# A 2-D spectral filter with a gate: products of both column halves in one tensor, stage 6 in two row tiles

## The chip, the cores and the metric

The kernel runs on one core of one Trainium2 chip. The metric is device time in microseconds of one execution. The core has a matrix engine (PE, with a weight-load stream of its own that the profile calls PEld), three elementwise engines (DVE, ACT, POOL), a queue that mostly issues transfers (SP), and 16 DMA engines. They run side by side and wait for each other through semaphores. Products of PE go to PSUM, eight banks of 512 float32 values on each of 128 partitions; everything else lies in SBUF.

## The reference

The input `x` is one matrix of 2048 rows and 1024 columns in bfloat16. Two filters A and B, each with a real and an imaginary weight of 2048 x 513, are applied to its 2-D spectrum, and a gate per row mixes the two results. The reference calls the same function twice, with A's weights and with B's, on the same `x`:

```
g = _sigmoid((x * gate_w).sum(-1, keepdims=True))
X = jnp.fft.rfft2(x.astype(jnp.float32), axes=(-2, -1))
X = X * (w_r + 1j * w_i)
y = jnp.fft.irfft2(X, s=(S, D), axes=(-2, -1)).astype(jnp.bfloat16)
return g * a + (1 - g) * b        # a: y with A's weights, b: y with B's
```

## The kernel before, in words

All transforms are matrix products with constant matrices, and the 2048 rows are split as 32 x 64 (row = 64 n1 + n2). The stages:

- Stages 1 and 2 load and fold `x` (`fold`), and transform it along n1 (`stage1`) and along the columns (`fold3`, `stage2`).
- Stage 4 (`stage4`) transforms along n2. It runs in 16 steps. Step i belongs to one half `hf` of the column frequencies and to one block `p` of two row frequencies; `SEQ` gives the order of the (hf, p) pairs. Each step leaves a spectrum tile X(i) in the buffer `XF`, copied out of PSUM by ACT (by DVE in steps 3 and 7). `swap` then copies X(i) to `MM` by DMA with neighbouring partitions exchanged, so that real and imaginary parts can be multiplied crosswise. POOL issues the swaps of steps 0 to 8, SP those of steps 9 to 15. There are six buffers (`NX`) for X and for its swapped copy.
- `product` multiplies X(i) (`sw` 0) or its swapped copy (`sw` 1) by the weights on DVE. The weights lie in `WA`, 64 rows (32 row frequencies for A, 32 for B) of 514 values, each row seen as two column halves of 257. With `sw` 0 the result goes to a second tensor `WB`, with `sw` 1 it goes over the weights in `WA`. One product covers both column halves of its columns. `ORDER` lists which products are put into DVE's queue after each step; entries are (step, sw, first half-block, half-blocks, steps). A half-block is 64 of the 128 columns of a `hf`.
- Weights come in six key groups (`wload`, keys 0 to 5: row frequencies in blocks 0, 1-3, 4-7, 8-11, 12-13, 14-15), 44 transfers issued by SP in that order. `product` waits for the key of its block. `save512` moves the column 512 of the weights out of the way and puts column 256 in its place; its second call (k = 1) reads the keys 1 to 5. It is called after step 9's products.
- Stage 5 (`group_mm`, `group_out`) transforms back along n2: 32 groups of 16 matmuls. Group g handles 8 columns; groups 1 to 15 and then 0 use `hf` 0, groups 16 to 31 use `hf` 1. Groups 1 to 7 need the lower half-blocks of all eight `hf` 0 products, groups 8 to 15 the upper ones, and likewise for `hf` 1. Step 14 stands ahead of group 1, step 15 behind the second group done. The result Z goes to `WB`, out of PSUM by ACT, a few by DVE.
- The gate: `row_sums` and `zsum` give the row sums of x times `gate_w`, ACT takes the sigmoid, and `gate_mask` writes it in two versions, one for each column half, with zeros at the other half's partitions. `rbgen` multiplies the constant `U5` by it, 1024 values for each of 16 r, half of them zero.
- Stage 6 (`stage6_mm`) transforms back along n1, mixing A and B: for each of 16 values of r, 16 matmuls with Z as weights and the scaled constant as moving operand. The contraction runs over 128 partitions (filter, row frequency, column half); the zeros keep the two column halves apart. Its output Y goes to `WA`.
- Stage 7 (`stage7`) transforms back along the columns. In the plain form PE works on half of the columns that the full form has, and ACT, DVE and POOL unfold them by sums and differences (POOL L837). The `half` form (r = 5, 9, 12) does one of the two unfoldings on PE, the `full` form (r = 14, 15) both; these leave POOL out. Outputs go to a ring of six buffers (`NOU`) and from there to memory by SP.

The order on each engine is the order of the `P.add` calls, written by hand, and every engine works strictly in that order. The class `Prog` derives the waits from keys: `r` reads, `w` writes, `a` adds to a key's writers. The lines that matter most here are these two loops (L676 to L687):

```
    for i in range(STEP5):
        step(i)
        ...
        products(i)
        if i in (1, 9):
            save512(i // 8, 0)
            save512(i // 8, 1)
```

Of the kernel before, what the change touches and what calls it, by code (L numbers as in the profile page):

```python
# [10 lines left out]
RW, HW = 514, 257  # L11
RWS = (528, RW)
# [13 lines left out]
def make_consts():  # L26
# [83 lines left out]
    l2, sl_, f = row % 2, (row // 2) % 32, row // 64  # L110
# [11 lines left out]
    SM[:, 1], SM[:, 2] = l2 == 0, l2 == 1  # L122
# [112 lines left out]
def bass_gated_mix__spectral_gfnet__spectral_gfnet__prompt_kernel(nc, A_x, A_w_r, A_w_i, B_x, B_w_r, B_w_i, gate_w, out):  # L235
# [7 lines left out]
    WA = sb("WA", 64 * RW)  # L243
    WB = sb("WB", 64 * RWS[0])
    FT = sb("FT", 16384)
    XF = sb("XF", 9216)
    MM = sb("MM", 6144)
    F2 = sb("F2", 2048)
    EO = sb("EO", 1024)
# [8 lines left out]
    VD = sb("VD", 1024)  # L258
# [4 lines left out]
    WT = (WB, WA)  # L263
# [32 lines left out]
    def xloc(c):  # L296
        return WT[c // 2], ((c % 2) * 32 + 24) * RWS[c // 2]

    XPARTS = {0: ((0, 1), (1, 1), (2, 2)), 1: ((0, 2), (2, 2)), 2: ((0, 2), (2, 2)), 3: ((0, 2), (2, 2))}
    XALL = [("x", c, q0) for c in range(4) for q0, n in XPARTS[c]]  # L300
# [25 lines left out]
    def wload(key, t0, t1):  # L326
        n = t1 - t0 + 1
        runs = ((t0, 2 * t0, n, 1), (32 - t0, 2 * t0 + 1, n, -1)) if t0 else ((0, 0, 2, 16),)
        for k0, s0, n, st in runs:
            for f in range(2):  # L330
                for ri in range(2):
                    src = wsrc[f, ri]
                    s = AP(src.tensor, src.offset + k0 * 513, [[32 * 513, 64], [st * 513, n], [1, 513]])
                    d = sl(WA, (f * 32 + s0) * RW, [(2 * RW if t0 else RW, n), (1, 513)], p0=ri, np_=64, pstep=2)
                    dma("sp", f"w{key}", d, s, a=[("W", key)] + XALL * (t1 >= 12))
        for t in range(t0, t1 + 1):
            need[t] = key
# [81 lines left out]
    NX = 6  # L419
# [6 lines left out]

    def fblock(cmb, j, t):
        if cmb in (1, 2):
            return sl(FT, cmb * 4096 + j * 2048 + t * 128, [(1, 128)])
        if t < 4:  # L430
            return sl((EO, VD)[t // 2], cmb // 3 * 512 + j * 256 + t % 2 * 128, [(1, 128)])
        return sl(FT, cmb * 4096 + j * 2048 + (t - 4) * 128, [(1, 128)])

    def ekeys(i, cs, s):
        return [("E", i, cs, s)] + ["VD"] * (i == 1)

    def fold3(i, css=(0, 1)):

        n = len(css)
        for s, op in enumerate((ALU.add, ALU.subtract)):  # L440
            src = [sl(FT, 12288 * css[0] + j * 2048 + i * 256, [(12288, n), (1, 256)]) for j in range(2)]
            dst = sl(FT, 12288 * css[0] + s * 2048 + (i - 2) * 256, [(12288, n), (1, 256)]) if i > 1 else sl((EO, VD)[i], 512 * css[0] + 256 * s, [(512, n), (1, 256)])
            P.add("dve", lambda e, dst=dst, src=src, op=op: e.tensor_tensor(out=dst, in0=src[0], in1=src[1], op=op),
                  r=[("F1a" if i < 2 else "F1", cs, j) for cs in css for j in range(2)] + [("FR", i, j) for j in range(2)],
                  w=[("E", i, cs, s) for cs in css] + [("FR", i - 2, s)] * (i > 1), a=["VD"] * (i == 1))
# [28 lines left out]
    def stage4(i):  # L474
# [12 lines left out]
        if i in (3, 7):  # L487
# [10 lines left out]
    def product(i, sw, h0=0, n=2, ni=1):  # L498

        hf, p = SEQ[i]  # L500
        steps = range(i, i + ni)
        assert all(SEQ[k] == (hf, p + k - i) and Xk(k) == Xk(i) + k - i for k in steps)
        xt, xo, xk = (MM, XSo(i), "XS") if sw else (XF, Xo(i), "X")
        at = lambda k: sl(WT[k], 4 * p * RWS[k] + 128 * hf + 64 * h0, [(32 * RWS[k], 2), (RWS[k] // 2, 8 * ni), (1, 64 * n)])
        P.add("dve", lambda e: e.tensor_tensor(out=at(sw), in0=sl(xt, xo + 64 * h0, [(0, 2), (128, 8 * ni), (1, 64 * n)]), in1=at(1), op=ALU.mult),  # L505
              r=[(xk, Xk(k)) for k in steps] + [("c256", p > 0)] * hf + [("W", need[t]) for t in range(2 * p, 2 * (p + ni))],
              a=[("prod", sw, hf, h) for h in range(h0, h0 + n)])
# [23 lines left out]
    def row_sums():  # L531
        vt = sl(VD, 0, [(1, 1024)]).bitcast(f32)
        P.add("dve", lambda e: e.tensor_tensor(out=vt, in0=sl(CL, VCo, [(1, 512)]), in1=sl(GSB, 0, [(0, 32), (2, 16)]), op=ALU.mult),
              r=["CV", "GSB"], w=["VD"])
        P.add("dve", lambda e: e.tensor_reduce(AT[:], vt.rearrange("p (n t) -> p n t", t=16), axis=mybir.AxisListType.X, op=ALU.add),
              r=["VD"], w=["AT"])
        P.add("dve", lambda e: e.tensor_copy(AB[:], AT[:]), r=["AT"], w=["AB"])

    def save512(k, part):

        s0, n = ((0, 4), (4, 28))[k]
        at = lambda l: sl(WA, s0 * RW + l, [(32 * RW, 2), (RW, n)])
# [12 lines left out]

    GMo = lambda r: (XF, 7168 + r * 256) if r < 8 else (MM, 4096 + (r - 8) * 256)

    def zsum(us):
        for k, u in enumerate(us):
            for n in range(16):  # L560
# [4 lines left out]
                  r=[bank(2 * u), bank(2 * u + 1), "SM"], **({"a" if k else "w": [("CS", 0), ("CS", 1)]}))  # L565

    def gate_mask(hf):
        t, o = GMo(8 * hf)
        for h in range(2):
            P.add("dve", lambda e, h=h: e.tensor_scalar(  # L570
                out=sl(t, o + h * 32, [(64, 32), (1, 32)]), in0=sl(XF, 1024 * hf, [(32, 32), (1, 32)]),
                scalar1=SM[:, 1 + h:2 + h], scalar2=None, op0=ALU.mult),
                r=[("CS", hf), "SM"], w=[("GM", hf, h), ("XS" if hf else "X", 4), ("XS" if hf else "X", 5)])


    def col0(u, sw):
        t = WT[sw]
# [4 lines left out]
        for q, (tt, to, st) in enumerate(((t, 0, RWS[sw]), (PST, sw * 64, 1))):  # L582
# [7 lines left out]
        P.add("act", lambda e: e.activation(sl(t, 0, [(RWS[sw], 64)]), ps(o0, [(1, 64)]), ACT.Copy),  # L590
# [3 lines left out]
    RBS = [(FT, (4 + k) * 2048 + 1024, []) for k in range(4)] + [(F2, 1024 * k, ["F2"]) for k in range(2)]  # L594
    RBS += [(XF, 1024 * k, [("CS", k)]) for k in range(3)] + [(XF, 3072 + 1024 * k, [("X", k)]) for k in range(4)]
    RBS += [(MM, 1024 * k, [("XS", k)]) for k in range(4)]

    def rbgen(r, eng, after=()):
        t, o, k = RBS[r]
        g, go = GMo(r)  # L600
        return P.add(eng, lambda e: e.tensor_tensor(
            out=sl(t, o, [(256, 4), (64, 4), (32, 2), (1, 32)]),
            in0=sl(FT, U5o + (r // 2) * 2048 + (r % 2) * 512, [(128, 4), (32, 4), (0, 2), (1, 32)]),
            in1=sl(g, go, [(0, 4), (64, 4), (32, 2), (1, 32)]), op=ALU.mult),
            r=["U5", ("GM", r // 8, 0), ("GM", r // 8, 1)], w=[("RB", r)] + k, after=[last2] + list(after))

    def group_mm(u, g, qs, at):
        hf = g // 16
        for q in qs:
            l0 = 8 * g + q  # L610
            o = ps(u * 1024 + at(q) * 128, [(1, 128)])
            for ab in range(2):
                deps = [("prod", ab, hf, g // 8 % 2), "CL"] + [("col0", ab)] * (g == 0)
                P.add("pe", lambda e, o=o, l0=l0, ab=ab: e.matmul(  # L614
                    o, sl(WT[ab], l0, [(RWS[ab] // 2, 128)]), sl(CL, KIo[ab], [(1, 128)]), start=(ab == 0), stop=(ab == 1)),
                    r=deps, w=[bank(2 * u + at(q) // 4)])

    def group_out(u, g, eng, q0, n, st, at, keys):
        src = ps(u * 1024 + at * 128, [(1, 128), (128, n)])
        dst = sl(WB, 8 * g + q0, [(RWS[0] // 2, 128), (st, n)])  # L620
# [36 lines left out]
    def step(i):  # L657
# [5 lines left out]
        if i == 15:  # L663
# [3 lines left out]
    ORDER = (((0, 0),), ((1, 0),), (), ((2, 0), (3, 0)), ((0, 1), (4, 0)), ((1, 1),), (), ((2, 1), (3, 1)),  # L667
             ((5, 0, 0, 2, 2), (4, 1), (5, 1, 0, 2, 2), (7, 0), (7, 1)), ((8, 0, 0, 1), (8, 1, 0, 1), (8, 0, 1, 1)), ((8, 1, 1, 1), (9, 0, 0, 2, 2)), ((9, 1, 0, 2, 2),), ((11, 0, 0, 2, 2),),
             ((11, 1, 0, 2, 2),))
# [38 lines left out]
    product(13, 0, 0, 2, 2)  # L708
    star_products()
# [3 lines left out]
    for a in ((13, 1, 0, 2, 2), (15, 0, 0, 1), (15, 1, 0, 1), (15, 0, 1, 1), (15, 1, 1, 1)):  # L713
        product(*a)
    row_sums()
# [8 lines left out]
    for n, g in enumerate(range(16, 32)):  # L724
        if n == 14:
            last_groups([spare(), spare()])
        elif n < 14:
            group(spare(), g, "dve" if n == 1 else "act")
        if n == 1:
            zsum([spare(), spare()])  # L730
            gate_mask(0)
            gate_mask(1)
            for _ in range(12):
# [6 lines left out]
    Yo, PQo = 0, 16384  # L740
    EOo = PQo + NPQ * 2048
    OUo = EOo + 2 * 1024
    assert OUo + NOU * 1024 <= 64 * RW

    def stage6_mm(r, bs, pis):
        b0 = 6 * (r % 2)
        t6, o6, _ = RBS[r]
        for b in bs:
            for pi in pis:
                for cp in range(2):  # L750
                    n = cp * 64 + 16 * b + r
                    lh = sl(WB, n * (RWS[0] // 2) + pi, [(2, 128)])
                    rh = sl(t6, o6 + cp * 512 + b * 64, [(256, 2), (1, 64)])
                    o = ps(b0 * 512 + b * 256 + pi * 128, [(1, 128)])
                    P.add("pe", lambda e, o=o, lh=lh, rh=rh, cp=cp: e.matmul(o, lh, rh, start=(cp == 0), stop=(cp == 1)),  # L755
                          r=[("Z", pi), ("RB", r)], w=[bank(b0 + b // 2)])

    def stage6(r, mm=True):
        b0 = 6 * (r % 2)
        if mm:  # L760
            stage6_mm(r, range(4), range(2))
        for k in range(2 if r == 0 else 1):
            n = 2 if r == 0 else 4
            src = ps((b0 + k) * 512, [(32, 8), (1, 32), (256, n)])
            dst = sl(WA, Yo + r * 128 + 2 * k, [(2048, 8), (4, 32), (1, n)])
            kw = dict(r=[bank(b0 + k + q) for q in range(n // 2)], a=[("Y", r)], after=[last5])
# [5 lines left out]
    HALF = (5, 9, 12)  # L772
    pqc = 0

    def stage7(r):
        nonlocal pqc
        full, half = r >= 14, r in HALF
        b0 = 6 * (r - 14) if r >= 14 else 4 - 2 * (r % 2)
        oo = OUo + (r % NOU) * 1024
        es = sl(WA, EOo + (r % 2) * 1024, [(1, 1024)]).bitcast(f32)  # L780

        def mm(col, c0, n, ri, pi, h, k, last):
            lh = sl(WA, Yo + (pi * 4 + ri * 2 + h) * 2048 + r * 128, [(1, 128)])
# [4 lines left out]
        def ods(s, k, n):  # L788
            return sl(WA, oo + 1023 * s + 512 * (1 - 2 * s) * k, [(512 * (1 - 2 * s), n), (1 - 2 * s, 256)])
# [11 lines left out]
        if full:  # L801
# [3 lines left out]
            for k0, n, bk in ((0, 2, b0),) if r == 14 else ((0, 1, b0), (1, 1, 4)):  # L805
                for k in range(4):
                    mm(bk * 512, k0, n, 0, k // 2, k % 2, k, 3)
                finals(k0, n, bk, WA, EOo + (r % 2) * 1024, [("EO", r % 2)])
        elif half:
# [7 lines left out]
            for s, op in enumerate((ALU.add, ALU.subtract)):  # L817
                P.add("dve", lambda e, s=s, op=op: e.tensor_tensor(out=sl(MM, to + s * 512, [(1, 512)]).bitcast(f32),
                                                                   in0=ps((b0 + 1) * 512, [(1, 256)]), in1=es[:, :256], op=op),
                      r=[("EO", r % 2), bank(b0 + 1)], w=[("T", r % 2, s), ("GM", 1, 0), ("GM", 1, 1)])  # L820
            finals(0, 2, b0, MM, to, [("T", r % 2, 0), ("T", r % 2, 1)])
        else:
# [7 lines left out]
            pq = PQo + pk * 2048  # L830
            for s, op in enumerate((ALU.add, ALU.subtract)):
                P.add("dve", lambda e, s=s, op=op: e.tensor_tensor(out=sl(WA, pq + s * 1024, [(1, 1024)]).bitcast(f32), in0=ps(b0 * 512, [(1, 512)]),  # L832
                                                                   in1=es, op=op),
                      r=[("EO", r % 2), bank(b0)], w=[("PQ", pk, s)], after=[last5])
            pv = sl(WA, pq, [(1, 2048)]).bitcast(f32).rearrange("p (a b c) -> p a b c", a=2, b=2)
# [6 lines left out]
        if r < 15:  # L842
            return [store("act" if r == 14 else "sp", f"o{r}", outv[:, r, :], sl(WA, oo, [(1, 1024)]), (0, 1))]
# [84 lines left out]
```

## Time and profile before

| | |
|---|---|
| median of 3 runs | 122.58 us (122.23 to 122.69) |
| profiled execution | 122.14 us, of which the span from first to last instruction is 120.1 us |
| PE / weight loads | 114.1 us busy (95%) / 95.9 us (80%) |
| DVE / ACT / POOL | 99.5 us (83%) / 99.0 us (82%) / 38.4 us (32%) |
| granted PE clock | 0.996 |
| DMA | 26.1 MB, mean 217 GB/s |

Busy times are shares of the whole span; the stages have different limits. Matmuls are pipelined, so a matmul's "busy" (219 ns for 128 columns) is its time in the pipeline, and the pace at which they follow each other is read from the chain or from start times. "L505" is line 505 of the kernel. In the groups an operation is shown with its output and inputs by the program's names. An idle time in brackets is the time that the engine sat before the instruction, and behind the arrow stands what ended it.

### The profile page before, as it was taken

To read this page: it belongs to the slowest core of one execution; us is meant where nothing else is said; L and a number is where in the kernel's file an instruction comes from. 1 tells how busy PE (TensorE), PEld (TensorE's weight loads), DVE (VectorE), ACT (ScalarE), POOL (GpSimd) and SP (SyncE) were. 2 spreads that over 40 slices of the span, in tenths; PEclk is the share of its full clock that TensorE was granted. 3 is DMA by queue.
4 is the path that set the end of the run, shared out by engine and by line. 5 is a ranking of instruction groups with operands and counts; after the bars stand their busy time and mean duration, and the time that the engine had idled before them with its cause. 6 is when DMAs were issued, how large, how long until landed. Compare 5 with 4: busy or idle time off the path is not lost.

```text
span 120.1 us, 3690 instructions
## 1 busy us (share of the span) xinstructions
PE 114.1 (95%) x1556; PEld 95.9 (80%) x1556; DVE 99.5 (83%) x160; ACT 99.0 (82%) x119; POOL 38.4 (32%) x47
## 2 busy tenths in 40 slices
PE   6998999999999999999999999999999999999960
PEld 4676889787675675689999999999899979898630
DVE  0568999988999999999999949995695687787890
ACT  4249998999797999899999989999779868867710
POOL 1000010036575500000000000000029999999980
PEclk9999999999999999999999999999999999999998
DMA  2999999999999999832699500000000422434456
GB/s 84 328 394 421 415 331 366 349 350 352 361 369 364 360 370 368 321 137 85 162 392 394 199 0 5 0 5 0 0 5 8 158 96 93 175 124 160 160 222 215
DMA packets 17680, 26.11 MB, mean 217 GB/s; under 512 B 2112, under 2 KB 11072, under 8 KB 17664
## 3 DMA queue, kind: packets, MB, share of 16 engines
q1 hardware_dynamic: 16368, 23.00, 54.6%
q0 software_dynamic: 864, 2.36, 5.4%
q10 hardware_dynamic: 432, 0.52, 1.4%
q8 instruction: 12, 0.20, 0.7%
q14 instruction: 4, 0.03, 0.1%
HBM read 17.48 MB, written 4.19 MB: 180 GB/s over the span
## 4 chain that ended last, share of the span: by engine, by line
PE 59%; SPq 18%; DMA 9%; DVE 8%; issue 3%; ACT 1%; POOL 0%; DVEq 0%; POOLq 0%
PE PS L614 26%; SPq L290 18%; PE PS L785 14%; PE PS L755 11%; DMA WA<-in_B_w_i_dram 9%; DVE WA L505 3%; PE PS L304 3%; DVE WB L505 3%; PE PS L387 2%; DVE WA L796 1%; PE PS L561 1%; PE PS L482 1%; PE PS L588 1%; ACT WB L625 1%; DVEq L867 0%
## 5 line engine op out<-in xcount | busy, mean ns | idle before, releaser
L837 POOL TENSOR_TENSOR WA<-WA 128x512 bf16<-128x512 f32 x22 | 27.6, 1290 | 48.2 <-DVE WA L832 48.2
L614 PE MATMUL PS<-CL,WB 128*128 128x128 bf16 x256 | 31.8, 226 | 0.0
L614 PE MATMUL PS<-CL,WA 128*128 128x128 bf16 x256 | 31.7, 223 | 0.1
L614 PEld LDWEIGHTS PS<-CL,WB 128*128 128x128 bf16 x256 | 31.3, 145 | 0.3 <-DVE WB L505 0.2
L614 PEld LDWEIGHTS PS<-CL,WA 128*128 128x128 bf16 x256 | 31.3, 145 | 0.3 <-DVE WA L505 0.2
L625 ACT ACTIVATE WB<-PS 128x1024 bf16<-128x1024 f32 (+1 forms) x31 | 28.8, 1042 | 0.2 <-PE PS L614 0.2
L770 ACT ACTIVATE WA<-PS 128x1024 bf16<-128x1024 f32 (+1 forms) x16 | 15.8, 996 | 6.2 <-PE PS L755 6.1
L505 DVE TENSOR_TENSOR WB<-XF,WA 128x2048 bf16<-128x2048 bf16 (+2 forms) x14 | 19.3, 1384 | 1.0 <-ACT XF L490 0.5
L785 PE MATMUL PS<-FT,WA 128*128 128x256 bf16 (+1 forms) x132 | 19.3, 292 | 0.1
L505 DVE TENSOR_TENSOR WA<-MM,WA 128x2048 bf16<-128x2048 bf16 (+2 forms) x14 | 19.2, 1385 | 0.0
L482 PE MATMUL PS<-XF,CK 128*128 128x512 bf16 (+1 forms) x72 | 17.5, 356 | 0.2 <-ACT XF L490 0.2
L832 DVE TENSOR_TENSOR WA<-PS,WA 128x512 f32<-128x512 f32 x22 | 14.2, 686 | 4.2 <-PE PS L755 1.9
L471 ACT ACTIVATE XF<-PS 128x1024 bf16<-128x1024 f32 x16 | 16.7, 1052 | 1.1 <-PE PS L465 1.0
L490 ACT ACTIVATE XF<-PS 128x1024 bf16<-128x1024 f32 x14 | 14.7, 1050 | 1.4 <-PE PS L482 0.6
L387 PE MATMUL PS<-MM,XF 128*128 128x256 bf16 x128 | 15.4, 280 | 0.3 <-DVE XF L348 0.3
L387 PEld LDWEIGHTS PS<-MM,XF 128*128 128x128 bf16 x128 | 12.5, 100 | 3.3 <-DVE XF L348 1.4
L785 PEld LDWEIGHTS PS<-FT,WA 128*128 128x128 bf16 x132 | 12.3, 98 | 3.3 <-DVE WA L768 0.2
L290 POOL DMA_DIRECT2D MM<-XF x18 | 9.9, 550 | 14.3 <-PE PS L482 8.7
L398 ACT ACTIVATE FT<-PS 128x1024 bf16<-128x1024 f32 (+2 forms) x15 | 13.1, 1012 | 0.9 <-PE PS L387 0.9
L348 DVE TENSOR_TENSOR XF<-WB 128x512 bf16<-128x512 bf16 (+1 forms) x20 | 6.0, 366 | 5.9 <-DMA WB<-in_A_x_dram 5.9
L456 PEld LDWEIGHTS PS<-F,FT 128*128 128x128 bf16 x128 | 8.4, 98 | 3.1 <-ACT FT L398 0.2
L456 PE MATMUL PS<-F,FT 128*128 128x128 bf16 x128 | 10.2, 219 | 0.0
(77 smaller groups left out, 134.1 us busy)
## 6 DMA issues: line engine op xcount, KB each, us to landing
out_dram<-WA SPq DMA_DIRECT2D x14, 256.0 KB, 2.2
MM<-XF POOLq DMA_DIRECT2D x18, 128.0 KB, 5.3
WA<-in_A_x_dram SPq DMA_DIRECT2D x4, 512.0 KB, 8.3
FT<-c_U SPq DMA_DIRECT2D x1, 2048.0 KB, 8.5
MM<-XF SPq DMA_DIRECT2D x14, 128.0 KB, 3.2
WB<-in_A_x_dram SPq DMA_DIRECT2D x3, 512.0 KB, 5.9
WA<-in_A_w_r_dram SPq DMA_DIRECT2D x4, 256.5 KB, 5.8
WA<-in_A_w_i_dram SPq DMA_DIRECT2D x4, 256.5 KB, 6.2
```

What stands on the lines that cost most here:

```text
L290: return P.add(eng, lambda e: e.dma_start(dst, src), dma=name, **kw)
L387: P.add("pe", lambda e, o=o, lh=lh, rh=rh, s=s: e.matmul(o, lh, rh, start=(s == 0), stop=(s == 1)), r=[("xf", c % 2, q, h, s ^ j), ("M", c ...
L456: P.add("pe", lambda e, o=o, cs=cs, j=j, t=t, rh=rh: e.matmul(o, fblock(1 + cs, j, t), rh, start=(j == 0), stop=(j == 1)), r=[("F1a" if p ...
L471: P.add("act", lambda e: e.activation(dst, src, ACT.Copy), **kw)
L482: P.add("pe", lambda e, o=o, kind=kind, pm=pm, m=m, rh=rh: e.matmul(o, sl(CK, fbo(kind, pm, m), [(1, 128)]), rh, start=(m == 0), stop=(m = ...
L490: P.add("act", lambda e: e.activation(dst, src, ACT.Copy), **kw)
L505: P.add("dve", lambda e: e.tensor_tensor(out=at(sw), in0=sl(xt, xo + 64 * h0, [(0, 2), (128, 8 * ni), (1, 64 * n)]), in1=at(1), op=ALU.mul ...
L614: P.add("pe", lambda e, o=o, l0=l0, ab=ab: e.matmul(o, sl(WT[ab], l0, [(RWS[ab] // 2, 128)]), sl(CL, KIo[ab], [(1, 128)]), start=(ab == 0) ...
L625: P.add("act", lambda e: e.activation(dst, src, ACT.Copy), r=b, a=keys)
L770: P.add("act", lambda e, s=src, d=dst: e.activation(d, s, ACT.Copy), **kw)
L785: P.add("pe", lambda e: e.matmul(ps(col, [(1, n * 256)]), lh, rh, start=(k == 0), stop=(k == last)), r=[("Y", r), "DI"] + ["DJ"] * (full o ...
L837: P.add("pool", lambda e, s=s, op=op: e.tensor_tensor(out=ods(s, 0, 2), in0=pv[:, :, 0, :], in1=pv[:, :, 1, :], op=op), r=[("PQ", pk, 0), ...
```

## The change

One tensor `W` of 128 rows of 520 values (`RP`) takes the place of `WA` and `WB`. Rows 0 to 63 hold the weights. A product now covers one column half (`kind` "A0", "B0", "A1", "B1": A from X, B from its swapped copy, 0 and 1 the column half). Half 0 goes to rows 64 to 127, half 1 over the weights in rows 0 to 63, A at column 0 and B at column 257. Since A1 and B1 overwrite weights that the other products of the step read, they get waits on them. There are now 64 products' worth of work, less those put together, in a new `ORDER`; `save512` keeps its place behind step 9's entry. X and its swapped copies get seven buffers, and ACT copies X(7) out.

With rows 0-63 and 64-127 the column half is the upper digit of the partition, so stage 6 takes each half by itself: two matmuls on 64 partitions and 64 columns, to two banks, where one on 128 partitions and 128 columns stood. The zeros, `gate_mask` and half of each scaled constant fall away, and all 16 constants are made after group 19. Stage 6 runs for two rows together ahead of the stage 7 of every odd r. The `half` form of stage 7 takes r = 2, 7, 10, 13 and the `full` form r = 5, 14, 15. Small buffers move; `x` lies in rows 96 to 127 of `W`.

```
-RW, HW = 514, 257
-RWS = (528, RW)
+HW, RP = 257, 520
...
-    WA = sb("WA", 64 * RW)
-    WB = sb("WB", 64 * RWS[0])
+    W = sb("W", 128 * RP)
...
-    NX = 6
+    NX = 7
...
-        if i in (3, 7):
+        if i == 3:
             P.add("dve", lambda e: e.tensor_copy(dst, src), **kw)
...
-        at = lambda k: sl(WT[k], 4 * p * RWS[k] + 128 * hf + 64 * h0, [(32 * RWS[k], 2), (RWS[k] // 2, 8 * ni), (1, 64 * n)])
-        P.add("dve", lambda e: e.tensor_tensor(out=at(sw), in0=sl(xt, xo + 64 * h0, [(0, 2), (128, 8 * ni), (1, 64 * n)]), in1=at(1), op=ALU.mult),
-              r=[(xk, Xk(k)) for k in steps] + [("c256", p > 0)] * hf + [("W", need[t]) for t in range(2 * p, 2 * (p + ni))],
-              a=[("prod", sw, hf, h) for h in range(h0, h0 + n)])
+        sw, h = "AB".index(kind[0]), int(kind[1])
+        rows = lambda o: sl(W, o + 4 * p * RP + 128 * hf + 64 * h0, [(32 * RP, 2), (RP, 4 * ni), (1, 64 * n)])
+        src = [("W%d" % h, hf, m, k) for m in steps for k in range(h0, h0 + n)]
+        over = [("W%d" % sw, hf, m, k) for m in steps for k in range(h0, h0 + n)] if h else []
+        P.add("dve", lambda e: e.tensor_tensor(out=rows((1 - h) * 64 * RP + sw * HW), in0=sl(xt, xo + 128 * h + 64 * h0, [(0, 2), (256, 4 * ni), (1, 64 * n)]),
+                                               in1=rows(h * HW), op=ALU.mult),
+              r=[(xk, Xk(k)) for k in steps] + [("c256", p > 0)] * (hf * h) + [("W", need[t]) for t in range(2 * p, 2 * (p + ni))] + [k for k in src if k not in over],
+              w=over, a=[("prod", sw, hf, h) for h in range(h0, h0 + n)])
...
-    ORDER = (((0, 0),), ((1, 0),), (), ((2, 0), (3, 0)), ((0, 1), (4, 0)), ((1, 1),), (), ((2, 1), (3, 1)),
-             ((5, 0, 0, 2, 2), (4, 1), (5, 1, 0, 2, 2), (7, 0), (7, 1)), ((8, 0, 0, 1), (8, 1, 0, 1), (8, 0, 1, 1)), ((8, 1, 1, 1), (9, 0, 0, 2, 2)), ((9, 1, 0, 2, 2),), ((11, 0, 0, 2, 2),),
-             ((11, 1, 0, 2, 2),))
+    each = lambda *a: lambda kinds: tuple((a[0], kinds[k:k + 2]) + a[1:] for k in range(0, len(kinds), 2))
+    rest = lambda *a: each(*a)("A0B0A1B1")
+    ORDER = (((0, "A0"),), ((1, "A0"),), (), ((3, "A0"), (2, "A0")), ((0, "B0"), (4, "A0"), (0, "A1")))
+    ORDER += tuple(((k + 1, "B0"), (k, "B1"), (k + 1, "A1")) for k in range(4))
+    ORDER += tuple(((k, "A0"), (k, "B0"), (k - 1, "B1"), (k, "A1")) for k in (5, 6))
+    lo7, lo8, up7, up8 = (each(k, c, 1) for c in range(2) for k in (7, 8))
+    ORDER += (lo7("A0B0") + ((6, "B1"),) + lo7("A1"), lo8("A0B0") + lo7("B1") + lo8("A1B1") + up7("A0B0") + up8("A0B0") + up7("A1") + up8("A1") + up7("B1") + up8("B1"), rest(9))
...
-                    lh = sl(WB, n * (RWS[0] // 2) + pi, [(2, 128)])
-                    rh = sl(t6, o6 + cp * 512 + b * 64, [(256, 2), (1, 64)])
-                    o = ps(b0 * 512 + b * 256 + pi * 128, [(1, 128)])
...
+                    for h in range(2):
+                        lh = sl(W, n * RP + pi, [(2, 128)], p0=64 * h, np_=64)
+                        rh = sl(t6, o6 + cp * 256 + b * 32, [(128, 2), (1, 32)], p0=64 * h, np_=64)
+                        o = ps((b0 + h) * 512 + pi * 256 + b * 32, [(128, 2), (1, 32)])
...
-    HALF = (5, 9, 12)
+    HALF, FULL = (2, 7, 10, 13), (5, 14, 15)
...
     for r in range(16):
-        for q in {0: (), 1: (2,), 2: (3, 4)}.get(r, (r + 2,) if r < 14 else ()):
+        pair = (r + 1, r + 2) if r % 2 and r < 14 else ()
+        for q in pair:
+            stage6_mm(q, range(4), range(2))
+        for q in pair[:1]:
             stage6(q)
         late += stage7(r)
-        if rb:
-            rbgen(rb.pop(0), "dve")
+        for q in pair[1:]:
+            stage6(q)
```

## The prediction

> **What bounds the kernel now.** I read the table of stages first (busy time in windows of 10 us), then the chain that ended last, then the vector and PE timelines around its joints, the DMA issues and the groups by form.
>
> ```profile
> 0.00:10.00 10.00, 8.89 (x54) 6.15 (x54) 4.10 (x15) 4.48 (x6) 0.55 (x6) 1.00 0.80 284
> ...
> 40.00:50.00 10.00, 9.77 (x137) 6.03 (x135) 9.83 (x9) 10.00 (x13) 1.09 (x2) 1.00 1.04 361
> 50.00:60.00 10.00, 9.97 (x155) 9.55 (x156) 9.97 (x8) 9.23 (x12) 0.00 (x0) 1.00 0.48 145
> ...
> 100.00:110.00 10.00, 10.00 (x129) 8.93 (x127) 8.03 (x14) 7.92 (x11) 10.00 (x9) 1.00 0.36 133
> ```
>
> Columns: window, length, busy us of PE, weight loads, DVE, ACT, POOL, granted clock, DMA share, GB/s. Up to 50 us DVE, ACT and DMA are all full; later PE, and at the end POOL too. The clock is 1.00, so no price here needs a clock factor.
>
> ```profile
> 50.03 1.13 PE PS L614 x15
> ...
> 70.43 13.67 PE PS L614 x224
> 84.09 0.02 issue
> 84.12 0.76 ACT WB L625
> ...
> 106.72 0.89 PE PS L755 x16
> 107.62 0.87 PE PS L785 x8
> 108.49 0.89 PE PS L755 x16
> 109.39 1.30 PE PS L785 x8
> 110.69 0.89 PE PS L755 x16
> 111.58 3.48 PE PS L785 x20
> ```
>
> From 50.03 the end is set by PE alone: stage 5 (L614) to 84.0, then per output row r one stage 6 (L755, 0.89) and one stage 7 (L785: 0.87 plain, 1.30 half, 1.74 full, eight 512-wide matmuls at 0.217).
>
> ```profile
> 40.74 2.31 DVE L505 TENSOR_TENSOR WB<-XF,WA 128x4096 bf16<-128x4096 bf16 x1 [0.17 <-DMA WA<-in_B_w_i_dram]
> 42.97 3.45 DVE L505 TENSOR_TENSOR WA<-MM,WA 128x2048 bf16<-128x2048 bf16 x2
> 46.33 1.23 DVE L505 TENSOR_TENSOR WB<-XF,WA 128x2048 bf16<-128x2048 bf16 x1
> 47.48 1.23 DVE L505 TENSOR_TENSOR WA<-MM,WA 128x2048 bf16<-128x2048 bf16 x1
> 48.66 0.70 DVE L505 TENSOR_TENSOR WB<-XF,WA 128x1024 bf16<-128x1024 bf16 x1
> 49.27 0.70 DVE L505 TENSOR_TENSOR WA<-MM,WA 128x1024 bf16<-128x1024 bf16 x1
> 49.88 0.69 DVE L505 TENSOR_TENSOR WB<-XF,WA 128x1024 bf16<-128x1024 bf16 x1
> 50.49 0.21 DVE L545 COPY W<-WA 128x56 bf16<-128x56 bf16 x1
> ```
>
> This is what releases 50.03: the last lower-half products, 48.66 to 49.97. The copy of column 512 (L545), which needs all weights, comes behind them.
>
> ```profile
> 42.50 0.61 SPq L290 DMA_DIRECT2D WA<-in_B_w_i_dram  x1
> ```
> ```profile
> WA<-in_B_w_r_dram SPq DMA_DIRECT2D x1, 128.2 KB, 5.5
> WA<-in_B_w_i_dram SPq DMA_DIRECT2D x1, 128.2 KB, 6.1
> ```
>
> The last weight DMA (key 5) is issued at 42.50 and lands 6.1 later, at 48.6: just before the product at 48.66 that needs it, so nothing waits.
>
> **The change, part by part.**
>
> *Products and the column-512 copy.* Prices start to start: 1024 elements 0.61 (48.66, 49.27, 49.88), 2048 elements 1.15 (46.33, 47.48), 512 elements about 0.35 (L443 512-wide, 0.42 with 0.08 overlapped). A 2048-wide product becomes two of 1024 (1.22). In the new DVE queue the A product of step 3 comes first after DVE's copy of X(3); that copy stays, 29.75 to 30.98. From 31.0 there are 21 products of 1024 before `save512(1)`: 21 x 0.61 = 12.8, so DVE arrives at 43.8. The swaps it needs land 5.0 to 5.9 after POOL's issue (issues from 25.87 to 40.30), key 3 at 40.65 against its use at 31.0 + 17 x 0.61 = 41.4; neither adds a wait. But `save512(1)` reads keys 1 to 5 and is now ahead of steps 6 to 8, where before it stood behind them. It waits until 48.6: 4.8 us of idle DVE. Nothing in the change moves the loads: the same 44 weight DMAs in the same order on SP, and the dropped dependence on x's readers was long satisfied.
>
> Behind it, before group 1 may start: the two copies 0.4, five products of 1024 (3.05) and eight of 512 (2.8, the last one waiting for its predecessor, +0.1), end of the last 0.1: 6.4. Lower half done at 55.0, against 49.97: **+5.0**. Bounds: +0.4 if the weights were already there at 43.8 (43.8 + 6.4 = 50.2), +5.8 if they land 0.8 later.
>
> Who waits: ACT's copy of X(14) now reuses X(7)'s buffer, whose last reader is the upper A1 product of step 7, five products of 0.35 after 55.0, so 56.8. ACT stands in line there, X(14) is out at 57.8, and stage 4 of step 15 on PE, due after two groups (55.0 + 2 x 0.98 + 0.1 = 57.1), starts at 57.8: **+0.7** (0 to 1.0). The other DVE deadlines hold: 36 products remain behind the lower half (16 of 512, 16 of 1024, 4 of 2048: 20 us, with row sums, waits and PST 23, to 78); groups 16 need the lower ones at 72.4 while PE gets there at 73.2; the row sums end at 74 against zsum at 75.2.
>
> *ACT* takes X(7)'s copy over from DVE, 0.9, where it waited 0.50 + 0.18 for it: +0.2, hidden behind the DVE wait (without that cover it would cost 0.2). DVE takes two stage-5 copies instead of one, ACT two half ones less; ACT's 0.91 per copy already fits under PE's 0.98 per group: nothing. Masks (4 x 0.47) and half of each scaled constant (16 x 0.3) leave DVE where PE sets the time: nothing.
>
> *Stage 5* loads weights at a stride of 1040 bytes instead of 528 and 514. Both old strides go at 61 ns a pair (13.67/224), so I take no difference; each 1 ns would be 0.5 us either way.
>
> *Stage 6.* 256 matmuls of 128 columns become 512 of 64 columns on 64 partitions, two by two on different partitions and banks. No row shows two at once. Ends for a pair: one after the other at the 29 ns of L561 (64 columns, 32 in 0.93), 58 ns; side by side, 29 ns. The four 15- and 1-column matmuls of L523 (0.10 for four, 25 ns) show that a narrower one gains nothing. So the stage costs 14.9 or 7.4, before 16 x 0.89 = 14.2: +0.6 or -6.8. I take side by side: the two of a pair share no operand partition and no bank, which is all that the trace shows them to need beside the queue.
>
> [...]
>
> Stage 6 runs in eight blocks, so PE goes 16 times between full matmuls and half ones. If each crossing waits for the matmul in flight, it costs 219 ns (busy, L755) less 56 (pace), 0.16: 0 to 2.6, I take 1.3. [...]
>
> *Stage 7.* Before 11 x 0.87 + 3 x 1.30 + 2 x 1.74 = 16.95, after 9 x 0.87 + 4 x 1.30 + 3 x 1.74 = 18.25: +1.3 on PE. POOL loses 4 of 22 operations of 1.25, 27.5 to 22.5.
>
> Sum for both stages on PE: 7.4 + 1.3 + 18.25 = 27.0 against 31.2. Per plain pair of rows PE then needs about 2.9 and ACT 2 x 0.92 + 2 x 0.5 = 2.84, and POOL ends no earlier than 4.2 (its first operands) + 22.5 = 26.7: no slack, so I give 1.2 back to waits: **-3.0**. Ends: -5.2 (no crossing cost, no waits) and +4.5 (one after the other, full crossings).
>
> Sum: 5.0 + 0.7 - 3.0 = +2.7. The profiled execution took 122.14 (span 120.1) and lies 0.44 under the median of 122.58, to which I add it: 125.3. A shift below 0.5% (0.6 us) could not be told from no change.
>
> **The rivals.**
>
> *Tiles one after the other (slower still).* Stage 6 at 25 to 29 ns a matmul: 12.8 to 14.9, with 18.25 and 0 to 2.6 against 31.2: -0.2 to +4.5, middle +2.3; with +5.7: 130.6. For it: every PE row of this trace is one at a time at 25 ns or more. Against: none of them has separate partitions.
>
> *Weights in time (faster).* If key 5 lands by about 43.8, the lower half is done at 50.2, X(14) still costs up to 0.7, and 0.9 - 3.0 gives 120.5. It decides below a landing of about 46: from there the DVE delay is under the 3.0 gained at the end. Against: DMA is full (share 1.04) from 10 to 48 us, and the bytes are the same. For it: DVE's arrival at 43.8 is a sum; and if DVE came later the wait would shrink but the end would not move.
>
> *Both fail:* no wait, no overlap: 0.9 + 2.3, 125.8. *Another stage-5 pace:* 5 ns more a matmul on top of my forecast, 127.9.
>
> **How the numbers follow.** Forecast 0.46 (its own range 123.2 to 127), tiles in series 0.27, weights in time 0.13, both fail 0.07, stage-5 pace 0.07. Predicted 125.3. The range leaves out most of the faster case (0.11) and the top of the serial one (0.09): 121.4 to 131.0. Faster by over 0.5% is the faster case and a sliver of the forecast with nothing lost in stages 6 and 7: 0.14; within 0.5%: 0.07; slower 0.79.
>
> **What would show it.** The wait: an idle of about 4 us on DVE before the column-512 copy, released by a weight DMA, and the first stage-5 matmul near 55. The buffer: a PE idle of 0.7 before the stage-4 matmuls of step 15. The tiles: stage 6 of two rows in about 1.0 us of PE when side by side, 1.8 when in series; a gap of up to 0.16 at each change between stages 6 and 7. POOL: 18 operations, no longer full. I am wrong if DVE shows no wait there, if stage 5 leaves its 61 ns, or if ACT or POOL hold PE by more than about 2 us at the end.

## The result, and the profile after

The changed kernel takes 126.72 us (median of 4 runs, 126.06 to 127.04) against 122.41 us of the kernel before: ratio 1.035, 95% interval 1.030 to 1.040. It is slower, as forecast; the forecast was 125.3 in a range of 121.4 to 131.0. The profiled execution took 126.74 us, its span is 124.6 us, 4.5 more than before.

The chain that ended last, in order of time (start, length, what), shows two of the three places where the 4.5 comes together:

```profile
42.80 5.94 DMA W<-in_B_w_i_dram
48.83 0.22 DVE W L545
49.07 0.29 DVE W L547
49.36 5.33 DVE W L504 x12
54.72 0.45 DVE W L504
55.17 0.05 issue
55.22 1.82 PE PS L600 x15
...
57.12 1.76 PE PS L600 x16
58.88 1.33 PE PS L477 x4
60.21 10.70 PE PS L600 x176
...
77.52 13.72 PE PS L600 x224
```

First, stage 5 (L600, formerly L614) starts its run at 55.22 instead of 50.03, and ahead of that in the chain stands the transfer of the last weights. (A single first matmul of stage 5 goes a little earlier, at 54.74 here and at 49.76 before; the start of stage 5 means the run of the 15 others, here and below.) Second, its first matmuls are slow: 15 in 1.82 us where the kernel before had 15 in 1.13. The last 224 go at 13.72, the old pace (13.67). DVE's timeline shows the wait itself:

```profile
43.37 0.69 DVE L504 TENSOR_TENSOR W<-XF,W 128x1024 bf16<-128x1024 bf16 x1
48.83 0.21 DVE L545 COPY W<-W 128x56 bf16<-128x56 bf16 x1 [4.76 <-DMA W<-in_B_w_i_dram]
49.07 0.29 DVE L547 COPY W<-W 128x56 bf16<-128x56 bf16 x1
```

DVE is done with the product at 43.37 a little after 44 and then stands for 4.76 us until the weights of key 5 land. In the kernel before the same copy stood behind the last lower-half product, when they had landed.

The slow start of stage 5 is in the table of stages (window, length, busy PE, weight loads, DVE, ACT, POOL, granted clock, DMA share, GB/s):

```profile
50.00:53.00 3.00, 0.10 (x1) 0.11 (x2) 3.00 (x7) 1.18 (x2) 0.00 (x0) 0.98 0.29 109
53.00:56.00 3.00, 2.04 (x11) 0.95 (x11) 2.97 (x9) 0.76 (x1) 0.00 (x0) 0.50 0.37 130
56.00:59.00 3.00, 3.00 (x31) 2.82 (x30) 3.00 (x8) 2.05 (x4) 0.00 (x0) 0.50 0.02 5
59.00:62.00 3.00, 3.00 (x37) 2.39 (x36) 2.90 (x6) 2.69 (x3) 0.00 (x0) 0.88 0.27 90
```

PE did almost nothing from 50 to 53, and from 53 to 59 its granted clock is 0.50. What it waited for is in PE's timeline, at the stage-4 matmuls of step 14: the copy of X(13) by ACT (first line), and that copy waited for DVE, which was late.

```profile
51.82 1.02 ACT L485 ACTIVATE XF<-PS 128x1024 bf16<-128x1024 f32 x1 [3.43 <-DVE W L504]
```
```profile
52.90 1.04 PE L477 MATMUL PS<-XF,CK 128*128 128x512 bf16 x2 [3.74 <-ACT XF L485]
54.74 2.29 PE L600 MATMUL PS<-CL,W 128*128 128x128 bf16 x16 [0.81 <-DVE W L504]
```

The third place is a gain, in the last stages. Stage 6 is L748, stage 7 L777:

```profile
94.23 1.11 PE L748 MATMUL PS<-FT,W 64*128 64x64 bf16 x64
95.28 2.35 PE L777 MATMUL PS<-FT,W 128*128 128x256 bf16 x16
97.56 1.11 PE L748 MATMUL PS<-FT,W 64*128 64x64 bf16 x64
```

A block of 64 half-partition matmuls, two rows' worth, lasts 1.05 (94.23 to 95.28) where the kernel before spent 2 x 0.89. From the first stage-6 matmul to the end it is 91.16 to 124.6, 33.4 us, against 84.02 to 120.1, 36.1.

The balance, in spans: start of stage 5 55.22 - 50.03 = +5.2; stage 5 itself 91.16 - 55.22 = 35.9 against 34.0, +1.9; the rest 33.4 - 36.1 = -2.6. Sum +4.5.

### The profile page after: what moved, and what is told of

Its sections match the earlier page's. It is cut to its first block, busy times and chain, and to the rows that moved or that the text cites. A ratio compares the mean times of both kernels' runs of the same rounds, so it can differ in the third digit from the quotient of the medians.

```text
span 124.6 us, 4237 instructions
## 1 busy us (share of the span) xinstructions
PE 112.7 (90%) x1812; PEld 90.1 (72%) x1812; DVE 97.5 (78%) x202; ACT 99.6 (80%) x119; POOL 34.0 (27%) x43
## 3 DMA queue, kind: packets, MB, share of 16 engines
q1 hardware_dynamic: 16368, 23.00, 52.9%
## 4 chain that ended last, share of the span: by engine, by line
PE 35%; SPq 27%; POOL 11%; DVE 10%; issue 6%; DMA 5%; ACT 2%; POOLq 1%; DVEq 0%
SPq L284 27%; PE PS L600 26%; POOL MM L829 8%; DMA W<-in_B_w_i_dram 5%; DVE W L504 5%; PE PS L297 3%; POOL XF L829 3%; DVE MM L788 2%; DVE FT L824 2%; PE PS L380 2%; PE PS L477 1%; POOLq L860 1%; PE PS L748 1%; PE PS L777 1%; ACT W L761 1%
## 5 line engine op out<-in xcount | busy, mean ns | idle before, releaser
L600 PE MATMUL PS<-CL,W 128*128 128x128 bf16 x512 | 33.8, 230 | 1.0 <-DVE W L504 0.8
L600 PEld LDWEIGHTS PS<-CL,W 128*128 128x128 bf16 x512 | 33.0, 146 | 2.3 <-DVE W L504 2.0
L829 POOL TENSOR_TENSOR MM<-FT 128x512 bf16<-128x512 f32 x14 | 17.5, 1275 | 56.2 <-DVE FT L824 56.2
L611 ACT ACTIVATE W<-PS 128x1024 bf16<-128x1024 f32 (+1 forms) x30 | 29.0, 1007 | 1.2 <-PE PS L600 1.1
L504 DVE TENSOR_TENSOR W<-XF,W 128x1024 bf16<-128x1024 bf16 (+2 forms) x36 | 22.1, 632 | 1.2 <-ACT XF L485 1.1
L504 DVE TENSOR_TENSOR W<-MM,W 128x1024 bf16<-128x1024 bf16 (+2 forms) x36 | 22.0, 637 | 0.2
L777 PE MATMUL PS<-FT,W 128*128 128x256 bf16 (+1 forms) x132 | 20.0, 302 | 0.6 <-DVE W L759 0.4
L761 ACT ACTIVATE W<-PS 128x1024 bf16<-128x1024 f32 (+1 forms) x16 | 15.8, 994 | 3.1 <-PE PS L748 3.0
L777 PEld LDWEIGHTS PS<-FT,W 128*128 128x128 bf16 x132 | 12.1, 98 | 6.3 <-DVE W L759 0.6
L341 DVE TENSOR_TENSOR XF<-W 128x512 bf16<-128x512 bf16 (+2 forms) x34 | 11.4, 404 | 6.0 <-DMA W<-in_A_x_dram 5.9
L824 DVE TENSOR_TENSOR FT<-PS,XF 128x512 f32<-128x512 f32 x18 | 11.6, 684 | 2.4 <-ACT XF L784 2.1
```

Source lines behind the costliest of these rows:

```text
L504: P.add("dve", lambda e: e.tensor_tensor(out=rows((1 - h) * 64 * RP + sw * HW), in0=sl(xt, xo + 128 * h + 64 * h0, [(0, 2), (256, 4 * ni), ...
L600: P.add("pe", lambda e, o=o, l0=l0, ab=ab: e.matmul(o, sl(W, HW * ab + l0, [(RP, 128)]), sl(CL, KIo[ab], [(1, 128)]), start=(ab == 0), sto ...
L611: P.add("act", lambda e: e.activation(dst, src, ACT.Copy), r=b, a=keys)
L761: P.add("act", lambda e, s=src, d=dst: e.activation(d, s, ACT.Copy), **kw)
L777: P.add("pe", lambda e: e.matmul(ps(col, [(1, n * 256)]), lh, rh, start=(k == 0), stop=(k == last)), r=[("Y", r), "DI"] + ["DJ"] * (full o ...
L829: P.add("pool", lambda e, s=s, op=op: e.tensor_tensor(out=ods(s, 0, 2), in0=pv[:, :, 0, :], in1=pv[:, :, 1, :], op=op), r=[("PQ", pk, 0), ...
```

## The experiments

My theory after the result: the copy of column 512 holds DVE until the last weights land; the idle PE behind it costs a second time through the clock; the row tiles gain as forecast. The rivals are that the wait would only move if the copy did, that stage 5 is slower because of its new stride of 1040 bytes, that half-partition matmuls are cheap whatever stands beside them, and that another engine holds the last stages.

### The copy later

```
-        if i in (1, 9):
+        if i in (1, 12):
             save512(i // 8, 0)
             save512(i // 8, 1)
```

> The changed kernel, with the second column-512 copy called after step 12's products instead of after step 9's. If the copy's wait for the last weights is the cause: DVE goes on to step 8 without it, is held only by the landing at about 48.7, first stage-5 matmul near 50.7 instead of 55.2, no half clock, stage 5 in 34.0 to 34.7 instead of 35.9, and the whole 120.8 us (120.0 to 121.5). Rival, the wait moves: the swapped copies or the late readers of X(7) hold DVE or ACT instead, first stage-5 matmul at 53 or later, 124 or more. Rival, stage 5 is slower because of its 1040-byte stride and not because of the clock: stage 5 stays at 35.9, 122.2.

Measured: 121.68 us, ratio to the kernel before 0.995 (0.992 to 0.997). From its timeline of DVE:

```profile
47.87 0.43 DVE L504 TENSOR_TENSOR W<-XF,W 128x512 bf16<-128x512 bf16 x1
49.24 0.43 DVE L504 TENSOR_TENSOR W<-XF,W 128x512 bf16<-128x512 bf16 x1 [0.94 <-DMA W<-in_B_w_i_dram]
49.58 0.77 DVE L504 TENSOR_TENSOR W<-MM,W 128x512 bf16<-128x512 bf16 x2
```

and of PE:

```profile
49.48 0.60 PE L477 MATMUL PS<-XF,CK 128*128 128x512 bf16 x2 [0.21 <-ACT XF L485]
50.75 0.28 PE L600 MATMUL PS<-CL,W 128*128 128x128 bf16 x1 [0.66 <-DVE W L504]
51.22 1.12 PE L600 MATMUL PS<-CL,W 128*128 128x128 bf16 x15 [0.20 <-DVE W L504]
...
54.04 1.04 PE L477 MATMUL PS<-XF,CK 128*128 128x512 bf16 x4 [0.57 <-ACT XF L485]
```

The weights still hold DVE, at the first product that needs them, but for 0.94 instead of 4.76 us, and the run of stage 5 starts at 51.22 instead of 55.22 (its single first matmul at 50.75 instead of 54.74). PE is nowhere idle for more than 0.7 us there and the clock is 1.0 in the whole run. Moving two small copies is worth 5.0 us of 126.7: the place of the copy, not the new products, made the change slower. The time lies 0.2 above the range I gave for it, since the weights landed at 49.2 and not 48.7, stage 5 took 34.9 and not at most 34.7, and the stages from 6 on lasted 33.8 and not 33.4. The last line is the wait for X(14) that the prediction had priced at 0.7: it was invisible at half clock, and is back.

### The clock alone

The copy stays where the change has it; 19 matmuls of 512 columns, whose results nobody reads, keep PE busy.

```
+    def fill(n):
+        for _ in range(n):
+            P.add("pe", lambda e: e.matmul(ps(512, [(1, 512)]), sl(CK, 0, [(1, 128)]), sl(CK, 0, [(1, 512)]), start=True, stop=True),
+                  r=["CK"], w=[bank(1)])
+
+    fill(14)
     step(14)
+    fill(5)
     groups(1)
```

> The changed kernel with 14 and 5 matmuls of 512 columns, whose results nobody reads, put on PE ahead of the stage-4 matmuls of step 14 and ahead of group 1, where PE stands idle. DVE's wait stays. If the half clock in slices 18 and 19 comes from that idle time: clock 1.0 throughout, the first 31 matmuls of stage 5 in 1.9 instead of 3.6 us, the wait for X(14) (up to 0.7) comes back, stage 5 about 34.7 instead of 35.9, whole 125.5 us (124.9 to 126.0). Rival, the clock falls for another reason, or the loss is not the clock: 126.7.

Measured: 125.49 us, ratio to the kernel before 1.028 (1.024 to 1.032), against 126.72 without them. DVE's wait in this run, then the table of stages in windows:

```profile
48.31 0.21 DVE L545 COPY W<-W 128x56 bf16<-128x56 bf16 x1 [4.32 <-DMA W<-in_B_w_i_dram]
```
```profile
51.00:54.00 3.00, 2.68 (x12) 0.90 (x10) 3.00 (x9) 1.94 (x2) 0.00 (x0) 1.00 0.34 127
54.00:57.00 3.00, 2.60 (x37) 2.26 (x36) 2.97 (x10) 0.56 (x1) 0.00 (x0) 1.00 0.14 51
57.00:60.00 3.00, 2.48 (x29) 1.88 (x30) 2.93 (x7) 3.00 (x5) 0.00 (x0) 1.00 0.25 89
```

The clock stays at 1.00, and doing more work makes the kernel 1.2 us faster. DVE still waits, 4.32 us here (the weights landed 0.5 earlier in this execution), so this separates the two costs. In the changed kernel the slow stretch costs 1.82 - 1.13, 1.76 - 1.03 and 1.33 - 0.86, 1.9 us together; here 0.8 of it comes back, 0.56 of that as the wait for X(14). From the start of stage 5 to the end of step 15's stage 4 it is 3.86 us here (54.70 to 58.56) against 4.99 in the changed kernel (55.22 to 60.21) and 3.10 before, so the full clock is worth 1.1 us net of that wait, whenever the weights land. The stride of 1040 bytes costs next to nothing: all runs with it do the last 224 matmuls in 13.69 to 13.72, against 13.67 before.

When the half clock begins, counted from PE's last matmul, differs from run to run. In the changed kernel it begins 3.7 us after it and lasts 6.8 us, from 52.9 to 59.7, which is 5.0 us beyond the first matmul of stage 5. In the run with the old unfoldings (below) it begins 2.5 us after it, at 51.7 (clock 0.84 in that window), in an idle time of 3.17 us:

```profile
51.00:52.00 1.00, 0.00 (x0) 0.00 (x0) 1.00 (x4) 0.78 (x1) 0.00 (x0) 0.84 0.28 109
```
```profile
52.30 1.03 PE L477 MATMUL PS<-XF,CK 128*128 128x512 bf16 x2 [3.17 <-ACT XF L485]
```

It also ends earlier there, and in the run with the tiles in series: the four stage-4 matmuls of step 15 take 1.03 and 0.86 us in these runs, against 1.33 in the changed kernel, and the same stretch of stage 5 loses 1.6 and 1.4 us instead of 1.9: the price of such a wait differs from run to run.

### The tiles in series

```
-        for b in bs:
-            for pi in pis:
-                for cp in range(2):
-                    for h in range(2):
+        for h in range(2):
+            for b in bs:
+                for pi in pis:
+                    for cp in range(2):
```

> The changed kernel, with the loop over the two partition halves outermost in stage 6, so that neighbouring matmuls fall into the same half; the same 512 matmuls. If the two halves run side by side only when they alternate: 64 matmuls take 64 x 29 ns = 1.86 instead of 1.04 us, 8 x 0.82 = 6.5 more on PE, of which 1 to 2 fall into its present gaps: 131 to 133 us. Rival, a matmul over 64 partitions is cheap by itself (16 ns whatever its neighbour): no change, 126.7.

Measured: 130.14 us, ratio to the kernel before 1.064 (1.060 to 1.068). Its chain, then the chain of the changed kernel with the late copy:

```profile
97.58 1.68 PE PS L748 x64
99.26 1.85 PE PS L777 x16
101.12 1.68 PE PS L748 x64
```
```profile
103.17 1.04 PE PS L748 x64
104.21 2.28 PE PS L777 x16
106.49 1.04 PE PS L748 x64
```

The same 64 matmuls take 1.68 in series and 1.04 when the halves alternate. Two of a pair run side by side when they are neighbours in the queue, and in series they do not. The 1.68 are under the 1.86 that I expected because the edit does not keep the halves wholly apart: by the start times in the trace, matmuls of one half follow each other at 29 ns, the pace of L561, and only at the three places in a block where the half changes do they stand closer (seven intervals in 0.11 us instead of 0.20). Part of the 5.1 us more on PE (8 x 0.64) fell into gaps, so the loss is 3.4 us and not 4.3 to 6.3. From stage 6 to the end this run takes 37.2 us (90.41 to 127.6), more than the 36.1 of the kernel before: without the overlap these stages would have gained nothing.

### The old unfoldings

```
-    HALF, FULL = (2, 7, 10, 13), (5, 14, 15)
+    HALF, FULL = (5, 9, 12), (14, 15)
```

> The changed kernel with the unfoldings of the old one: half form at r = 5, 9, 12, full form at r = 14, 15. If POOL bounds the last stage of the changed kernel: 22 operations of 1.25 instead of 18, from about 96.0 to 124 or later, the stores behind them, 128 to 129 us. Rival, PE bounds it: PE loses 1.3 and the kernel gains about 1, 125.7. Rival, neither: within 0.5 of 126.7.

Measured: 127.83 us, ratio to the kernel before 1.045 (1.039 to 1.050), 1.1 above the changed kernel. POOL in this run, then in the changed kernel:

```profile
95.15 9.91 POOL L829 TENSOR_TENSOR MM<-FT 128x512 bf16<-128x512 f32 x8 [53.74 <-DVE FT L824]
105.01 2.51 POOL L829 TENSOR_TENSOR XF<-FT 128x512 bf16<-128x512 f32 x2
107.48 7.44 POOL L829 TENSOR_TENSOR MM<-FT 128x512 bf16<-128x512 f32 x6
114.88 4.94 POOL L829 TENSOR_TENSOR XF<-FT 128x512 bf16<-128x512 f32 x4
119.79 2.48 POOL L829 TENSOR_TENSOR MM<-FT 128x512 bf16<-128x512 f32 x2
```
```profile
110.08 4.98 POOL L829 TENSOR_TENSOR MM<-FT 128x512 bf16<-128x512 f32 x4 [1.27 <-DVE FT L824]
115.02 2.50 POOL L829 TENSOR_TENSOR XF<-FT 128x512 bf16<-128x512 f32 x2
117.48 2.50 POOL L829 TENSOR_TENSOR MM<-FT 128x512 bf16<-128x512 f32 x2
```

With the old sets POOL has no idle time after its start and bounds the end; with the new ones it has a gap, though the chain that ended last still runs through it, from 101.36 to 119.76. The intervals against the kernel before touch (1.039 to 1.050, and 1.030 to 1.040 for the changed kernel), and the span of this profile is only 0.2 longer, 124.8; but it reached stage 6 earlier, at 90.28 instead of 91.16, and from there it takes 34.5 us against 33.4. So the moved unfoldings are worth their 1.3 us of PE once stage 6 is short, though the run stays a little under what I had written for it (128 to 129).

### One row at a time

The kernel with the late copy, and stage 6 in the old order:

```
-        pair = (r + 1, r + 2) if r % 2 and r < 14 else ()
-        for q in pair:
-            stage6_mm(q, range(4), range(2))
-        for q in pair[:1]:
-            stage6(q)
+        for q in {0: (), 1: (2,), 2: (3, 4)}.get(r, (r + 2,) if r < 14 else ()):
+            stage6_mm(q, range(4), range(2))
+            stage6(q)
         late += stage7(r)
-        for q in pair[1:]:
-            stage6(q)
```

> The kernel with the late copy, and stage 6 for one row at a time as in the old order: about 15 blocks of half-partition matmuls instead of 8, so about 14 more crossings between full and half ones. If each crossing waits for the matmul in flight (0.16 us): up to 2.2 longer, 123.9; if a crossing costs nothing: 121.7. A value between gives the price, as far as ACT's changed order does not add its own waits.

Measured: 123.36 us, ratio to the kernel before 1.006 (1.004 to 1.009), so 1.7 over the paired order (121.68). Its chain:

```profile
102.25 0.57 PE PS L748 x32
102.82 0.98 PE PS L777 x8
103.80 0.57 PE PS L748 x32
104.37 0.98 PE PS L777 x8
```

32 half-partition matmuls take 0.57 and 64 take 1.04, so 32 more cost 0.47 (14.7 ns each) and a block has 0.10 on top. A plain stage 7 takes 0.98 instead of the 0.87 that it took between full matmuls: 0.11 for the way back. A crossing costs about 0.1 us each way. 14 more at that price are 1.5, near the 1.7 that was measured; waits that ACT's changed order may have added are in the rest.

### A version that beats both

The wait for X(14) comes from the late readers of X(7). The kernel with the late copy, and step 7's upper products ahead of step 8's lower ones, where DVE waits for the weights anyway:

```
-    ORDER += (lo7("A0B0") + ((6, "B1"),) + lo7("A1"), lo8("A0B0") + lo7("B1") + lo8("A1B1") + up7("A0B0") + up8("A0B0") + up7("A1") + up8("A1") + up7("B1") + up8("B1"), rest(9))
+    ORDER += (lo7("A0B0") + ((6, "B1"),) + lo7("A1"), up7("A0B0A1") + lo8("A0B0") + lo7("B1") + lo8("A1B1") + up8("A0B0") + up7("B1") + up8("A1B1"), rest(9))
```

> The kernel with the late copy, and step 7's upper A0, B0 and A1 products put ahead of step 8's lower ones, into the 0.94 us in which DVE waits there for the last weights. If the late readers of X(7) are what still holds PE after two groups (ACT idle 2.62 before the copy of X(14), PE idle about 0.8): X(14) is out by 51, no PE idle before step 15's stage 4, first stage-5 matmul unchanged at 51, whole 120.9 us (120.5 to 121.3) against 121.7. Rival, PE then waits elsewhere in stage 5 or the end is set by POOL: 121.4 to 121.8.

Measured: 121.35 us, ratio to the kernel before 0.989 (0.985 to 0.992). Its chain has no wait left between the groups and step 15's stage 4:

```profile
52.88 1.05 PE PS L600 x16
53.93 0.86 PE PS L477 x4
54.79 10.76 PE PS L600 x176
```

The time lies just above the range that I gave (120.5 to 121.3). Against the late copy alone the profile shows 0.4 us (span 119.5 against 119.9), not the 0.7 of the removed wait (from the second group to stage 4 it is 52.28 to 54.04 there and 52.74 to 53.77 here), because in this run stage 5 started at 51.66 and not at 51.22. Most of that shift belongs to the run: DVE's products ahead of the moved ones start 0.33 later already (42.67 against 42.34). The two ratios' intervals lie just apart (0.9925 to 0.9973 and 0.9853 to 0.9923), so the gain over the late copy is small and its size open.

## Why the prediction was right, point by point

- *DVE's wait.* Priced at 4.8 us of idle and +5.0 for the start of stage 5; measured 4.76 and +5.2. The arrival (43.8 forecast, about 44.0 measured), the landing (48.6; the copy ran at 48.83) and the products behind it held. The late copy shows that this is the cause: it returns 5.0 us, the clock's share included. (The lower bound of this term, +0.4, does not follow from its own figures: 50.2 against 49.97 is +0.2, which the faster rival uses.)
- *The buffer of X(7), +0.7.* This term failed in this kernel. The mechanism is real (PE idle 0.57 in the run with the late copy, 0.56 in the one with fill matmuls), but PE came to it late, at 58.88, when X(14) was out.
- *Stage 5 at its old pace.* The pace of 61 ns is right from the third group on. What the sum lacked is the clock: the prediction said that the granted clock was 1.00 and that no price needed a factor, and did not ask what the new idle time would do to it. I named the delayed copy of X(14), but not that X(13) waits for DVE too and leaves PE without work for 3.74 us. This cost 1.9 in place of 0.7; the fill matmuls, which keep the clock at 1.00, confirm it.
- *Stages 6 and 7, -3.0.* Measured -2.6. The choice of "side by side" was right (29.4 ns a pair, against ends of 29 and 58), the crossings cost 0.10 to 0.11 each where I took 0.08, sixteen of them 1.7 instead of 1.3. With that the allowance of 1.2 for waits comes out about right; POOL and ACT have little slack, as said. (The faster end of this term should read -5.5, not -5.2: 7.4 + 18.25 - 31.2.)
- *Tiles of 64 rows and 64 columns.* No row of the kernel before has a tile of 64 rows, so "side by side" was an estimate. A block of 64 takes 1.04 us in alternation, against 1.68 in series, and that decides for it: 29.4 ns a pair. A crossing costs 0.10 to 0.11 us, less than the 0.16 that I had worked out for one that waits for the matmul in flight.
- *The sum.* 5.0 + 0.7 - 3.0 = +2.7 was forecast, 5.2 + 1.9 - 2.6 = +4.5 came. By spans the sum was 1.8 low: 1.2 in stage 5, where the clock came in place of the buffer, 0.4 in the last stages, 0.2 in DVE's wait. By the times the forecast was 1.4 low, because it added the 0.44 by which the profile of the kernel before lay under its median, and the profiled execution of the changed kernel has no such offset. So part of the closeness is luck: a wait that did not occur stood in for 0.7 of the clock's 1.9, and the 0.44 covered some of the rest.
- *The faster rival*, weights in time, had the right direction: with the late copy the kernel takes 121.68 us, 0.7 less than the one before, against the 120.5 of the rival, which has no wait for the weights at all. It was put down to an earlier landing; moving the copy does most of the same.

## What to carry to other kernels

On an engine that works strictly in order, look at every instruction that an edit puts ahead of the old ones and ask what it waits for: two copies, half a microsecond together, harmless behind the products, cost 5 us ahead of them and hid a redesign that by itself gains 0.7. When an edit leaves PE without work for long, ask what the clock will do: 3.2 to 3.7 us without a matmul were enough here for half clock behind the gap, worth 1.6 to 1.9 us, and 0.8 us were harmless; no run lies between. Row tiles paid here for 64 columns, with the two halves in alternation and the full and half matmuls kept in large blocks.

## What the runs showed of the hardware that I had not expected

- In a stretch of 3.74 us without a matmul (3.17 with the old unfoldings) the granted clock fell to 0.50, 3.7 us after its start (2.5 there), and in the changed kernel it stayed there for 6.8 us, though stage-4 matmuls ran in between. With the late copy PE idled for up to 0.66 us in the same place and the clock was 1.0; behind an idle time of 0.82 us, in the version that beats both, 16 matmuls of stage 5 took 1.05 us, against 1.76 at half clock.
- Half-partition matmuls of 64 columns, each with its own weight load, follow each other at 14.7 ns on average in alternation, where the narrow ones of L523 need 25 ns. By the start times of the changed kernel's trace the two of a pair start 3 to 4 ns apart and the next pair about 26 ns later; their weight loads, 95 ns each, start 3 to 4 ns apart as well, so two loads run side by side.
- In one half they follow each other at 29 ns, like full matmuls of the same 64 columns (L561 of the kernel before): half the partitions alone make a matmul no shorter.
- Matmuls of 128 columns whose weight loads have strides of 514, 528 (before) and 1040 bytes all follow each other at 61 ns, against 56 in the old stage 6, whose neighbouring weight columns are 4 bytes apart (0.89/16). The profile gives 145 and 98 ns for such a load; that the stride is the reason was not tested.
